# Two accumulators and two query banks in PSUM as four tiles, and a reciprocal written back to PSUM

## The chip, the cores and the metric

The kernel runs on one core of one Trainium2 chip. The metric is the device time of one execution in microseconds; for the kernel before, the median of three runs is 2843.22 us (2841.27 to 2845.21).

## The reference

One token of a small decoder, batch 2: an attention layer with a cache, a gated GELU layer, and both once more with the same weights, each on a layer norm of `x` and added back to `x`. All numbers are float32.

```python
def _A_ref(x, k_cache, v_cache, wq, wo):          # x (2,1,576), caches (2,32,8192,128)
    q = (x @ wq).reshape(B, Sq, H, Dh).transpose(0, 2, 1, 3)
    scores = jnp.einsum("bhqd,bhkd->bhqk", q, k_cache) * (Dh ** -0.5)
    p = _softmax(scores, axis=-1)
    o = jnp.einsum("bhqk,bhkd->bhqd", p, v_cache)
    return o.transpose(0, 2, 1, 3).reshape(B, Sq, H * Dh) @ wo

def _B_ref(x, w_gate, w_up, w_down):              # 576 -> 4608 -> 576
    h = _gelu(x @ w_gate) * (x @ w_up)
    return h @ w_down

x = x + _A_ref(_layernorm(x), ...)
x = x + _B_ref(_layernorm(x), ...)
x = x + _A_ref(_layernorm(x), ...)
x = x + _B_ref(_layernorm(x), ...)
```

The two caches have 268 MB each and are read once in each attention layer, so nearly all of the traffic is cache.

## The kernel before

**Items and slots.** The attention of a layer is a list of items. A *pair* item is two heads of one batch element (30 of them), a *single* is one head (4: s0 to s3). Layer 0 takes the pairs, then the singles; layer 1 goes backward, and takes some of the singles' keys and values from where layer 0 left them in SBUF. A pair's keys are one load of 128 partitions x 16384 numbers, its values another. SBUF holds three slots of that size (`P0`, `P1`, `P2`), and the loads go round them in turn: keys of item n, values of item n, keys of item n+1, and so on. So the values of item n take the slot of the keys of item n-1, and the keys of item n+1 the slot of the values of item n-1.

**Loads.** A small planner (`Space`) keeps a list of loads in a fixed order and issues the next one on the SP queue (line 136 for caches) as soon as the program has reached the instruction that frees its slot: the last sum over a slot of keys, or the last matmul over a slot of values. On the chip the SP queue then waits for that instruction. The order of the loads is the order of the list.

**One item.** `query(n)` (line 452, TensorE) spreads the item's query over the partitions into bank `n % 2` of the PSUM tile `qp`. `multiply(n, unit)` (line 480, VectorE) multiplies a unit of the keys with it in place; a pair has five units, of two, two, two, one and one eighths. GpSimd adds the two halves of each product (line 484), and VectorE sums what is left (`add_up`, line 490). `peak`, `highest`, `softmax` and `total` find the maximum (501, 503, 508, 511), the exponentials (519, 523, ScalarE) and their sum over the partitions, a matmul into the PSUM tile `tot` (533). `values(n)` (551, TensorE) multiplies the exponentials with the values into bank `n % 2` of the PSUM tile `acc`. `invert` (541, 543) makes the reciprocal of the sum and the weights, `gather` (561, 563) picks the diagonal of the accumulator, `context` (571, 576) applies the weights.

**Order.** The order on each engine is the program's (a manual schedule). For a pair it is, in the loop over units k:

```python
made = multiply(n, unit)
if k == 0:  query(n + 1)              # the next item's query, after the first multiply
else:       add_up(*pending)
if k == 2:  invert(n - 1)
if k == 3:  gather(n - 1); context(n - 1)
...
# after the last unit
add_up(*pending); peak(n); highest(n); softmax(n); total(n); values(n)
```

So on TensorE the query of item n+1 stands behind the values matmuls of item n-1, and on VectorE the work on item n-1 that needs the values matmuls stands behind the fourth multiply of item n. For singles, the end of one item lies inside the next. The framework sets the semaphores: it lets an instruction wait for another where both touch a tile in a way that it sees as a conflict.

**Other uses of the two tiles.** The query projection of a layer goes through `acc`, and the gate and up products of the GELU layer take both banks of `acc` for one half and both of `qp` for the other (662); `copy` takes one bank with ScalarE (672) and the other with VectorE (673).

Of the kernel before, what the change touches and what calls it, by code (L numbers as in the profile page):

```python
# [9 lines left out]
F32 = mybir.dt.float32  # L10
AF = mybir.ActivationFunctionType
ALU = mybir.AluOpType
# [3 lines left out]
P = 128  # L16
# [3 lines left out]
DH = 128  # L20
# [5 lines left out]
HALF = P // 2  # L26
# [3 lines left out]
WIN = 2 * RW  # L30
# [4 lines left out]
BF = CF // 2  # L35
# [60 lines left out]
def decode_layers(ctx, tc, x_in, kc, vc, wq, wo, wg, wu, wd, out):  # L96
    nc = tc.nc
# [3 lines left out]
    work = ctx.enter_context(tc.tile_pool(name="work", bufs=2))  # L101
    once = ctx.enter_context(tc.tile_pool(name="once", bufs=1))
    psum1 = ctx.enter_context(tc.tile_pool(name="psum1", bufs=1, space=PSUM))
# [3 lines left out]
    space = consts.tile([P, END], F32, name="space")  # L107
    sp = Space()
    at_of = {}
# [12 lines left out]
    def done(key):  # L122
        sp.free(key)
        sp.pump()
# [194 lines left out]
    prz = consts.tile([P, 2, 32, 2, 4], F32, name="prz")  # L319
# [9 lines left out]
    spread = consts.tile([P, 8, B], F32, name="spread")  # L329
    chosen = consts.tile([P, 2, B], F32, name="chosen")  # L330

    acc = psum1.tile([P, 2, 512], F32, name="acc")
    qp = psum1.tile([P, 2, 512], F32, name="qp")
    xps = psum1.tile([P, 512], F32, name="xps")
    nc.vector.tensor_scalar(x, x, onerow, None, op0=ALU.add)
    nc.vector.memset(xps, 0.0)
    for s in range(2):
        nc.vector.memset(acc[:, s, :], 0.0)
        nc.vector.memset(qp[:, s, :], 0.0)

    wide = x.rearrange("p (q i) -> p q i", i=9)

# [26 lines left out]
    def norm(apart):  # L369

        every = psum2.tile([P, B * 24], F32, name="every", tag="small")
        nc.tensor.matmul(every, ones, apart.rearrange("p b c t -> p (b c t)"), start=True, stop=True)
        mv = work.tile([P, B, 2], F32, name="mv")
        for b in range(B):
            nc.vector.bn_aggr(mv[:, b, :], every[:, 24 * b:24 * b + 24])
        ve = work.tile([P, B], F32, name="ve")
        nc.vector.tensor_scalar_add(ve, mv[:, :, 1], EPS)  # L377
        rstd = work.tile([P, B], F32, name="rstd")
        nc.gpsimd.tensor_tensor(out=rstd, in0=ve, in1=mhalf, op=ALU.pow)  # L379
        shift = work.tile([P, B], F32, name="shift")  # L380
        nc.vector.scalar_tensor_tensor(shift, mv[:, :, 0], -1.0, rstd, op0=ALU.mult, op1=ALU.mult)
        k8 = pick.rearrange("p c g r -> p (c g) r")
        part = work.tile([P, 8, B], F32, name="part")
        nc.vector.tensor_mul(spread, k8[:, :, 0:B], rstd.unsqueeze(1).to_broadcast([P, 8, B]))
        nc.vector.tensor_mul(
            part, k8[:, :, B:RW].to_broadcast([P, 8, B]), shift.unsqueeze(1).to_broadcast([P, 8, B])
        )
        nc.vector.tensor_add(spread, spread, part)
        nc.vector.reduce_sum(
            chosen.rearrange("p g b -> p (g b)"), spread.rearrange("p (c g) b -> p (g b) c", c=4), axis=AX.X  # L390
        )

    def window(g, i):
        at = RW * (1 - g) + 32 * i
        return xt[:, at:at + WIN]

    both = xm[:, 3:5, :].rearrange("p k r -> p (k r)")
    only = [xm[:, k:k + 2, :].rearrange("p k r -> p (k r)") for k in (0, 1)]


    def attention(layer, items, apart):
        last = len(items) - 1
        qsb = once.tile([P, CQ], F32, name="qsb", tag="row")

        def queries(bank, lhs, at, start, stop):
            for c in range(4):
                nc.tensor.matmul(
                    bank[32 * c:32 * c + WIN, :], lhs, space[:, at + c * CQ:at + (c + 1) * CQ],
                    start=start, stop=stop,
                )  # L410

        if layer == 0:
            bank = acc[:, 0, :]
            for off, n in ((0, 3), (3, 3), (6, 2)):
                for u in range(off, off + n):
                    queries(bank, window(u % 2, u // 2), at_of["wq", 0, off] + (u - off) * HQ, u == 0, False)
                done(("wq", 0, off))
                if off == 0:
                    norm(apart)
            queries(bank, both, at_of["wq", 0, "m"], False, True)  # L420
            done(("wq", 0, "m"))
            nc.scalar.activation(qsb, bank, AF.Copy)
        else:
            for i in range(NW):
                queries(acc[:, 1, :], window(1, i), at_of["wq", 1, 1, i], i == 0, False)
                done(("wq", 1, 1, i))
                if i == 0:
                    norm(apart)
            queries(acc[:, 1, :], only[1], at_of["wq", 1, "m"], False, True)
            queries(xps, only[0], at_of["wq", 1, "m"], True, False)  # L430
            done(("wq", 1, "m"))
            nc.scalar.activation(qsb, acc[:, 1, :], AF.Copy)

        def rest_of_queries():
            for i in range(NW):
# [7 lines left out]
        S, peaks, low, osb, weights = {}, {}, {}, {}, {}  # L443
# [3 lines left out]
        def query(n):  # L447
            item = items[n]
            for e in range(2):
                h = item.h + (e if item.heads == 2 else 0)  # L450
                half, c = h // 16, (h // 4) % 4
                nc.tensor.matmul(  # L452
                    qp[HALF * e:HALF * e + HALF, n % 2, 0:DH],
                    chosen[32 * c:32 * c + WIN, half, item.b:item.b + 1].to_broadcast([WIN, HALF]),
                    qsb[32 * c:32 * c + WIN, (h % 4) * DH:(h % 4 + 1) * DH], start=True, stop=True,
                )
# [11 lines left out]
        def multiply(n, unit):  # L468
            item = items[n]
            lo, hi = unit  # L470
            if lo == 0:
                S[n] = work.tile([P, 128], F32, name="S")
            j = 16 * (hi - lo)
            at = base_of("k", item, lo)
            t = space[:, at:at + (hi - lo) * PART].rearrange("p (j d) -> p j d", d=DH)
            u = t
            if layer == 0 and lo < stays("k", item):
                at = at_of["scratch", item.name] + lo % 2 * PART
                u = space[:, at:at + PART].rearrange("p (j d) -> p j d", d=DH)
            nc.vector.tensor_tensor(  # L480
                out=u, in0=t, in1=qp[:, n % 2, 0:DH].unsqueeze(1).to_broadcast([P, j, DH]), op=ALU.mult
            )
            half = u[:, :, :DH // 2]
            nc.gpsimd.tensor_tensor(out=half, in0=half, in1=u[:, :, DH // 2:], op=ALU.add)  # L484
            return n, unit, half
# [51 lines left out]

        def invert(n):
            heads = items[n].heads
            rinv = work.tile([P, heads], F32, name="rinv")  # L540
            nc.vector.reciprocal(rinv, low.pop(n))
            weights[n] = work.tile([P, heads], F32, name="weights")
            nc.vector.tensor_mul(weights[n], of[:, 0:2] if heads == 2 else of[:, 2:3], rinv)  # L543

        def values(n):
            item = items[n]
            groups = item.rows // 4
            for g in range(groups):
                c = g % 4
                at = base_of("v", item, g // 4) + g % 4 * 4 * DH  # L550
                nc.tensor.matmul(  # L551
                    acc[32 * c:32 * c + 8, n % 2, :], prz[:, n % 2, g, :, :].rearrange("p e r -> p (e r)"),
                    space[:, at:at + 4 * DH], start=(g < 4), stop=(g >= groups - 4),
                )
                if g % 4 == 3 and (layer == 1 or g // 4 >= stays("v", item)):
                    done(key_of("v", item, g // 4))

        def gather(n):
            t = osb[n] = work.tile([P, DH], F32, name="osb")
            q = acc[:, n % 2, :].rearrange("p (r d) -> p r d", r=4)  # L560
            nc.vector.tensor_scalar_mul(t, q[:, 0, :], diag[:, 0:1])
            for r in range(1, 4):
                nc.vector.scalar_tensor_tensor(t, q[:, r, :], diag[:, r:r + 1], t, op0=ALU.mult, op1=ALU.add)  # L563
# [89 lines left out]
    def mlp(layer, apart):  # L653
        banks = acc, qp
        done_first = set()

        def products(half, lhs, at, stop):
            for s in range(2):
                for c in range(4):
                    key = half, s, c  # L660
                    lo = at + c * CF + s * BF
                    nc.tensor.matmul(  # L662
                        banks[half][32 * c:32 * c + WIN, s, 0:BF], lhs, space[:, lo:lo + BF],
                        start=key not in done_first, stop=stop,
                    )
                    done_first.add(key)
# [2 lines left out]

        def copy(half):  # L670
            t = o[half] = once.tile([P, 2, BF], F32, name="o", tag="row")
            nc.scalar.activation(t[:, 0, :], banks[half][:, 0, 0:BF], AF.Copy)  # L672
            nc.vector.tensor_copy(t[:, 1, :], banks[half][:, 1, 0:BF])  # L673

        def turned(half):
            t = o[half].rearrange("p s w -> p (s w)")
# [32 lines left out]
        if layer == 0:  # L709
# [14 lines left out]
            d = downs[0]  # L724
# [63 lines left out]
```

## Time and profile before

| what | value |
|---|---|
| median of three runs | 2843.22 us (2841.27 to 2845.21) |
| the profiled execution, time / span | 2843.0 us / 2841.2 us |
| granted TensorE clock, mean | 0.637 |
| read from HBM | 1153.18 MB, 406 GB/s over the span |
| busy: VectorE / GpSimd / TensorE | 2002.7 / 1173.6 / 955.8 us |

Layer 0's pairs end near 1264 us of the span, its singles near 1352; then come the output projection, the GELU layer and the next query projection, to about 1474; layer 1's singles and pairs, to about 2757; and the last projection and GELU layer. In the rows of the profile PE is TensorE's matmul, PEld its weight load, DVE is VectorE, ACT ScalarE, POOL GpSimd and SPq the queue on which the loads are issued. A row of the timeline has the start in us, the duration in us, engine, line, operation, output and input by name, and in a bracket the time for which the engine stood idle before it and what released it. Tile names come without their numbers.

### The profile page before, as it was taken

How to read it: one execution, taken by the hardware profiler on the slowest of the kernel's cores; microseconds unless marked ns; L12 is line 12 of the kernel's file. 1: busy time of each engine (PE TensorE's matmuls, PEld its weight loads, DVE VectorE, ACT ScalarE, POOL GpSimd, SP SyncE). 2: the span in 40 equal slices, each digit the busy share in tenths (PEclk: the TensorE clock that was granted, in tenths of full speed). 3: DMA queues.
4: the chain of work that ended last, by engine and by line, in shares of the span. 5: the costliest groups of instructions: out<-in, count | busy, mean ns of one | idle time of the engine just before them, and what ended most of it. 6: DMA issues, size and time to landing. Idle time of an engine off the chain costs nothing.

```text
span 2841.2 us, 18902 instructions
## 1 busy us (share of the span) xinstructions
PE 955.8 (34%) x7836; PEld 347.6 (12%) x7836; DVE 2002.7 (70%) x1330; ACT 93.1 (3%) x419; POOL 1173.6 (41%) x342
## 2 busy tenths in 40 slices
PE   1332333233223322334654332332233223323345
PEld 0110011011101110111211110111011001100123
DVE  4678777877777787768029778777777877787760
ACT  0000000000000000000000000000000000000000
POOL 2444444444444344434015444444444444444430
PEclk7665666666566656666666656665666566666668
DMA  9999999999999999997999999999999999999999
GB/s 428 427 428 402 427 400 413 410 416 401 413 415 409 404 412 416 412 392 311 379 350 380 440 414 416 416 412 400 427 400 413 400 428 400 414 399 427 399 417 389
DMA packets 30853, 1154.39 MB, mean 406 GB/s; under 512 B 3488, under 2 KB 3504, under 8 KB 5296
## 3 DMA queue, kind: packets, MB, share of 16 engines
q1 hardware_dynamic: 30744, 1153.19, 95.9%
q8 instruction: 61, 1.00, 0.1%
q14 instruction: 24, 0.20, 0.0%
q10 hardware_dynamic: 24, 0.01, 0.0%
HBM read 1153.18 MB, written 0.00 MB: 406 GB/s over the span
## 4 chain that ended last, share of the span: by engine, by line
DVE 26%; PE 14%; DMA 7%; issue 5%; POOL 2%; ACT 1%; POOLq 0%; SPq 0%; DVEq 0%
DVE space L480 11%; PE acc L551 10%; DVE S L490 9%; DVE weights L543 3%; DMA space<-in_B_w_down_dram 3%; POOL space L484 2%; DMA space<-in_B_w_gate_dram 2%; DVE osb L563 1%; DMA space<-in_A_k_cache_dram 1%; PE nb L511 1%; ACT prz L523 1%; DMA space<-in_A_wo_dram 1%; PE tot L533 1%; DMA space<-in_B_w_up_dram 1%; PE qp L452 0%
## 5 line engine op out<-in xcount | busy, mean ns | idle before, releaser
L484 POOL TENSOR_TENSOR space<-space 128x2048 f32<-128x2048 f32 (+1 forms) x332 | 1170.1, 3525 | 1439.7 <-DVE space L480 1397.3
L480 DVE TENSOR_TENSOR space<-space,qp 128x4096 f32<-128x4096 f32 (+1 forms) x332 | 1140.9, 3437 | 511.3 <-PE qp L452 413.7
L490 DVE TENSOR_REDUCE S<-space 128x32 f32<-128x2048 f32 (+1 forms) x332 | 594.4, 1790 | 85.7 <-POOL space L484 85.7
L551 PE MATMUL acc<-space,prz 128*8 128x512 f32 x4096 | 595.9, 746 | 0.0
L571 PE MATMUL po<-weights,osb 128*32 128x1 f32 x1024 | 59.5, 201 | 1260.3 <-DVE osb L563 1260.3
L571 PEld LDWEIGHTS po<-weights,osb 128*32 128x32 f32 x1024 | 54.1, 154 | 1278.3 <-DVE osb L563 1278.1
L551 PEld LDWEIGHTS acc<-space,prz 128*8 128x8 f32 x4096 | 114.8, 104 | 419.2 <-issue 409.5
L503 PE MATMUL mT<-ident,m 128*1 128x128 f32 x68 | 25.1, 369 | 384.5 <-DVE m L501 384.5
L543 DVE TENSOR_TENSOR weights<-of,rinv 128x2 f32<-128x2 f32 (+1 forms) x68 | 149.5, 2199 | 2.4
L511 PE MATMUL nb<-m,strip 1*128 1x1 f32 x256 | 64.5, 350 | 38.8 <-DVE m L508 38.8
L576 ACT COPY oT<-po 64x4 f32<-64x4 f32 (+1 forms) x68 | 10.7, 157 | 2028.0 <-PE po L571 2028.0
L563 DVE SCALAR_TENSOR_TENSOR osb<-acc,diag,osb 128x128 f32<-128x128 f32 x204 | 71.6, 351 | 7.3
L379 POOL TENSOR_TENSOR rstd<-ve,mhalf 128x2 f32<-128x2 f32 x4 | 2.8, 699 | 167.2 <-DVE ve L377 167.2
L511 PEld LDWEIGHTS nb<-m,strip 1*128 1x128 f32 x256 | 58.7, 313 | 57.6 <-DVE m L508 54.6
L533 PE MATMUL tot<-rs,strip 128*128 128x2 f32 x120 | 34.9, 360 | 77.2 <-ACT prz L523 77.2
L503 PEld LDWEIGHTS mT<-ident,m 128*1 128x1 f32 x68 | 5.4, 79 | 397.4 <-DVE m L501 366.1
L523 ACT ACTIVATE prz<-S,nbs 64x128 f32<-64x128 f32 (+1 forms) x136 | 53.4, 393 | 3.1
L452 PE MATMUL qp<-qsb,chosen 6*64 6x128 f32 x272 | 31.3, 308 | 26.2 <-DVE space L480 25.5
L533 PEld LDWEIGHTS tot<-rs,strip 128*128 128x128 f32 x120 | 29.8, 308 | 82.3 <-ACT prz L523 82.3
L508 DVE TENSOR_REDUCE m<-mT 1x2 f32<-1x128 f32 (+1 forms) x68 | 18.9, 278 | 28.3 <-PE mT L503 28.3
L673 DVE COPY o<-acc 128x288 f32<-128x288 f32 x2 | 0.9, 458 | 53.0 <-ACT o L672 53.0
L662 PE MATMUL acc<-space,xt 128*6 128x288 f32 x256 | 28.9, 588 | 26.3 <-DMA space<-in_B_w_up_dram 15.4
(89 smaller groups left out, 336.6 us busy)
## 6 DMA issues: line engine op xcount, KB each, us to landing
space<-in_A_k_cache_dram SPq DMA_DIRECT2D x6, 4096.0 KB
space<-in_A_wo_dram SPq DMA_DIRECT2D x16, 1152.0 KB
space<-in_A_v_cache_dram SPq DMA_DIRECT2D x3, 4096.0 KB
space<-in_B_w_down_dram SPq DMA_DIRECT2D x13, 864.0 KB
space<-in_A_wq_dram SPq DMA_DIRECT2D x10, 1024.0 KB
space<-in_B_w_gate_dram SPq DMA_DIRECT2D x8, 1152.0 KB
space<-in_B_w_up_dram SPq DMA_DIRECT2D x8, 1152.0 KB
space<-in_B_w_gate_dram SPq DMA_DIRECT2D x2, 4608.0 KB
```

The lines of the kernel that those rows point to most:

```text
L452: nc.tensor.matmul(qp[HALF * e:HALF * e + HALF, n % 2, 0:DH], chosen[32 * c:32 * c + WIN, half, item.b:item.b + 1].to_broadcast([WIN, HALF ...
L480: nc.vector.tensor_tensor(out=u, in0=t, in1=qp[:, n % 2, 0:DH].unsqueeze(1).to_broadcast([P, j, DH]), op=ALU.mult)
L484: nc.gpsimd.tensor_tensor(out=half, in0=half, in1=u[:, :, DH // 2:], op=ALU.add)
L490: nc.vector.tensor_reduce(out=S[n][:, 16 * lo:16 * hi], in_=half, axis=AX.X, op=ALU.add)
L503: nc.tensor.transpose(peaks[n], m, ident)
L511: nc.tensor.matmul(low[n], one_of[e] if heads == 2 else ones[0:1, :], m1[:, e:e + 1], start=(e == 0), stop=(e == heads - 1),)
L523: nc.scalar.activation(prz[rows_, n % 2, 0:item.rows // 4, e, :], s[rows_, 0:item.rows].rearrange("p (g r) -> p g r", r=4), AF.Exp, bias=n ...
L533: nc.tensor.matmul(tot, ones, rs[:, n % 2, :], start=True, stop=True)
L543: nc.vector.tensor_mul(weights[n], of[:, 0:2] if heads == 2 else of[:, 2:3], rinv)
L551: nc.tensor.matmul(acc[32 * c:32 * c + 8, n % 2, :], prz[:, n % 2, g, :, :].rearrange("p e r -> p (e r)"), space[:, at:at + 4 * DH], start ...
L563: nc.vector.scalar_tensor_tensor(t, q[:, r, :], diag[:, r:r + 1], t, op0=ALU.mult, op1=ALU.add)
L571: nc.tensor.matmul(po[lo + 32 * e:lo + 32 * e + 32, n % 2, i:i + 1], t[:, i::GH], w[:, e:e + 1], start=True, stop=True,)
```

## The change

`acc` and `qp`, one tile of two banks each, become lists of two tiles of one bank each; every use takes the same bank as before under its new name. [...] The order of the program is untouched. Second, `invert` writes the reciprocal over the sum in PSUM in place of a tile in SBUF, and the weights are made from there. The core of the diff:

```diff
-    acc = psum1.tile([P, 2, 512], F32, name="acc")
-    qp = psum1.tile([P, 2, 512], F32, name="qp")
+    acc = [psum1.tile([P, 512], F32, name="acc%d" % s) for s in range(2)]
+    qp = [psum1.tile([P, 512], F32, name="qp%d" % s) for s in range(2)]
...
                 nc.tensor.matmul(
-                    qp[HALF * e:HALF * e + HALF, n % 2, 0:DH],
+                    qp[n % 2][HALF * e:HALF * e + HALF, 0:DH],
...
             nc.vector.tensor_tensor(
-                out=u, in0=t, in1=qp[:, n % 2, 0:DH].unsqueeze(1).to_broadcast([P, j, DH]), op=ALU.mult
+                out=u, in0=t, in1=qp[n % 2][:, 0:DH].unsqueeze(1).to_broadcast([P, j, DH]), op=ALU.mult
             )
...
             heads = items[n].heads
-            rinv = work.tile([P, heads], F32, name="rinv")
-            nc.vector.reciprocal(rinv, low.pop(n))
+            rinv = low.pop(n)
+            nc.vector.reciprocal(rinv, rinv)
             weights[n] = work.tile([P, heads], F32, name="weights")
             nc.vector.tensor_mul(weights[n], of[:, 0:2] if heads == 2 else of[:, 2:3], rinv)
...
                 nc.tensor.matmul(
-                    acc[32 * c:32 * c + 8, n % 2, :], prz[:, n % 2, g, :, :].rearrange("p e r -> p (e r)"),
+                    acc[n % 2][32 * c:32 * c + 8, :], prz[:, n % 2, g, :, :].rearrange("p e r -> p (e r)"),
...
-            q = acc[:, n % 2, :].rearrange("p (r d) -> p r d", r=4)
+            q = acc[n % 2].rearrange("p (r d) -> p r d", r=4)
...
-            nc.scalar.activation(t[:, 0, :], banks[half][:, 0, 0:BF], AF.Copy)
-            nc.vector.tensor_copy(t[:, 1, :], banks[half][:, 1, 0:BF])
+            nc.scalar.activation(t[:, 0, :], banks[half][0][:, 0:BF], AF.Copy)
+            nc.vector.tensor_copy(t[:, 1, :], banks[half][1][:, 0:BF])
```

More of the change, by code (lines that the diff above doesn't have):

```diff
@@ L337, in decode_layers @@
     for s in range(2):
-        nc.vector.memset(acc[:, s, :], 0.0)
-        nc.vector.memset(qp[:, s, :], 0.0)
+        nc.vector.memset(acc[s], 0.0)
+        nc.vector.memset(qp[s], 0.0)
     wide = x.rearrange("p (q i) -> p q i", i=9)
@@ L412, in attention @@
         if layer == 0:
-            bank = acc[:, 0, :]
+            bank = acc[0]
             for off, n in ((0, 3), (3, 3), (6, 2)):
@@ L424, in attention @@
             for i in range(NW):
-                queries(acc[:, 1, :], window(1, i), at_of["wq", 1, 1, i], i == 0, False)
+                queries(acc[1], window(1, i), at_of["wq", 1, 1, i], i == 0, False)
                 done(("wq", 1, 1, i))
@@ L428, in attention @@
                     norm(apart)
-            queries(acc[:, 1, :], only[1], at_of["wq", 1, "m"], False, True)
+            queries(acc[1], only[1], at_of["wq", 1, "m"], False, True)
             queries(xps, only[0], at_of["wq", 1, "m"], True, False)
             done(("wq", 1, "m"))
-            nc.scalar.activation(qsb, acc[:, 1, :], AF.Copy)
+            nc.scalar.activation(qsb, acc[1], AF.Copy)
         def rest_of_queries():
@@ L662, in products @@
                     nc.tensor.matmul(
-                        banks[half][32 * c:32 * c + WIN, s, 0:BF], lhs, space[:, lo:lo + BF],
+                        banks[half][s][32 * c:32 * c + WIN, 0:BF], lhs, space[:, lo:lo + BF],
                         start=key not in done_first, stop=stop,
```

## The prediction

> **What bounds the kernel now.** First the busy shares and the transfer queue on the page, then the lists of waits, then one attention item in the timeline, then the stages side by side.
>
> ```profile
> PE 955.8 (34%) x7836; PEld 347.6 (12%) x7836; DVE 2002.7 (70%) x1330; ACT 93.1 (3%) x419; POOL 1173.6 (41%) x342
> q1 hardware_dynamic: 30744, 1153.19, 95.9%
> ```
>
> The second line says that the 16 DMA engines hold a packet 95.9% of the span, which looks like a kernel bound by its transfers and nothing else. The list of waits (microseconds in total, times, longest) says that VectorE also stops often, and the SP queue's own list says what the loads wait for:
>
> ```profile
> DVE space L480 <- PE qp L452: 413.7, 62, 11.5
> DVE space L480 <- DMA space<-in_A_k_cache_dram: 97.4, 54, 22.9
> SPq L136 <- DVE m L501: 1631.1, 61, 29.3
> SPq L136 <- PE qp L452: 723.4, 56, 13.2
> ```
>
> In the multiply (L480) VectorE waits four times as long for the query matmul (L452) as for the keys. Whether that matters depends on whether loads are issued late. Here is one item, from the end of one to the end of the next; the bracket is the idle time before the row and its releaser.
>
> ```profile
> 607.79 0.33 SPq L136 DMA_DIRECT2D space<-in_A_v_cache_dram  x1
> 607.80 0.29 DVE L501 TENSOR_REDUCE m<-S 128x1 f32<-128x128 f32 x1
> 608.55 0.28 DVE L508 TENSOR_REDUCE m<-mT 1x2 f32<-1x128 f32 x1 [0.46 <-PE mT L503]
> 610.32 4.42 DVE L480 TENSOR_TENSOR space<-space,qp 128x4096 f32<-128x4096 f32 x1 [1.49 <-DMA space<-in_A_k_cache_dram]
> 611.18 0.58 PE L533 MATMUL tot<-rs,strip 128*128 128x2 f32 x2 [1.29 <-ACT prz L523]
> 611.70 9.22 PE L551 MATMUL acc<-space,prz 128*8 128x512 f32 x64
> 620.85 0.43 PE L452 MATMUL qp<-qsb,chosen 6*64 6x128 f32 x4
> 620.99 0.33 SPq L136 DMA_DIRECT2D space<-in_A_k_cache_dram  x1
> 621.33 4.42 DVE L480 TENSOR_TENSOR space<-space,qp 128x4096 f32<-128x4096 f32 x1 [6.58 <-PE qp L452]
> 632.44 4.50 POOL L484 TENSOR_TENSOR space<-space 128x2048 f32<-128x2048 f32 x1 [2.03 <-DVE space L480]
> 634.39 0.16 DVE L541 RECIPROCAL rinv<-tot 128x2 f32<-128x2 f32 x1
> 634.58 2.38 DVE L543 TENSOR_TENSOR weights<-of,rinv 128x2 f32<-128x2 f32 x1
> 641.28 0.34 DVE L561 TENSOR_SCALAR osb<-acc,diag 128x128 f32<-128x128 f32 x1
> 648.76 0.33 SPq L136 DMA_DIRECT2D space<-in_A_v_cache_dram  x1
> 651.39 4.42 DVE L480 TENSOR_TENSOR space<-space,qp 128x4096 f32<-128x4096 f32 x1 [1.59 <-DMA space<-in_A_k_cache_dram]
> ```
>
> Follow it. At 607.80 the keys of the previous item are summed. The softmax chain leads to the values matmuls (611.70 to 620.92); the query for the item *after* stands behind them on TensorE (620.85). VectorE has done this item's first multiply by 614.74, and its second multiply, which reads the other query bank, stops for 6.58 us until that query is written. From 621.33 VectorE runs on to 648.76, and only then is the next value load issued, because its slot was the keys' slot. So 13.53 us (607.80 to 621.33) plus 27.43 us (to 648.76) close a ring of 40.96 us through VectorE and TensorE. The load at 648.76 comes only 2.63 us before the keys ahead of it are used; the queue almost runs dry once an item. The stages show the price (window, its length, busy times with instruction counts, clock, DMA share, GB/s):
>
> ```profile
> 84.73:123.44 38.71, 8.75 (x71) 3.44 (x63) 30.81 (x19) 1.31 (x6) 18.23 (x5) 0.57 1.00 434
> 84.73:201.21 116.48, 29.98 (x239) 11.03 (x227) 92.44 (x54) 3.44 (x16) 54.73 (x15) 0.61 1.00 432
> 201.21:1224.00 1022.79, 308.87 (x2273) 107.10 (x2274) 770.78 (x451) 32.08 (x147) 456.26 (x125) 0.63 0.96 410
> 1224.00:1342.00 118.00, 48.75 (x329) 17.66 (x329) 96.39 (x81) 6.22 (x30) 55.84 (x21) 0.67 0.83 348
> 1342.00:1480.00 138.00, 89.22 (x1031) 32.93 (x1035) 17.40 (x60) 3.08 (x11) 4.87 (x4) 0.67 0.94 362
> 1480.00:1579.00 99.00, 43.78 (x247) 15.37 (x243) 87.59 (x72) 5.80 (x28) 52.42 (x20) 0.66 0.94 391
> 1695.95:2720.51 1024.56, 309.42 (x2275) 107.60 (x2275) 770.41 (x450) 33.49 (x154) 456.17 (x125) 0.62 0.97 410
> 2720.51:2841.20 120.69, 73.33 (x1075) 38.75 (x1075) 39.12 (x56) 2.69 (x12) 18.95 (x6) 0.78 0.95 404
> ```
>
> POOL runs five times an item, so the second row holds 3 items (15), the third and the seventh 25 each (125). In the second, with loads issued ahead, an item takes 116.48 / 3 = **38.83 us** at 432 GB/s and a DMA share of 1.00. In the two long ones it takes 1022.79 / 25 = 40.91 and 1024.56 / 25 = 40.98 us. The long stages are bound by the ring, not by the transfers.
>
> **Part 1: four PSUM tiles.** Instruction order is the same on every engine in the built program of the changed kernel. What differs is waits. With two banks in one tile, the second multiply waits for the write of the other bank, and that query waits for the first multiply; with separate tiles both waits are absent. The query's own reader, the next item's first multiply, comes some 25 us later. Without the 6.58 us stop, VectorE's round is 1.04 us (607.79 to the end of L508 at 608.83), 4.42 us (first multiply) and 27.43 us: 32.89 us. That is below 38.83, so the transfers become the bound. What is late next? The value load is then issued 38.83 - 4.42 - 27.43 = 7.0 us before the keys ahead of it are used. The key load waits for the values matmuls to free their slot; these end 13.13 us after the keys are summed (607.79 to 620.92), so it goes out 7.0 + 19.4 - 13.1 = 13.3 us before the values ahead of it have landed (19.4 us is half an item). Both leads exceed the 2.63 us of now. The two long stages give 25 x (40.91 - 38.83) = **52.0** and 25 x (40.98 - 38.83) = **53.8** us.
>
> A wait on TensorE is added at line 561 (the gather of the weighted values) and one at the reciprocal, since the second multiply no longer covers them. Behind line 561 stand the last multiply and sums, and so the value load. It costs nothing: the gather runs at 641.28, and the values matmuls it needs ended at 620.92, 20.4 us before; without the stop of 6.58 and the 2.2 us of part 2 some 11.6 us are left, and more once VectorE waits for keys.
>
> **Part 2: the reciprocal into PSUM.** The small multiply at L543 takes 2.38 us for 128x2 numbers: it begins at 634.58 and ends at 636.96, just when GpSimd's operation (632.44 + 4.50 = 636.94) ends. With GpSimd idle it is far shorter:
>
> ```profile
> 1345.26 0.16 DVE L543 TENSOR_TENSOR weights<-of,rinv 128x1 f32<-128x1 f32 x1
> ```
>
> Its form afterwards, one operand in SBUF and one in PSUM, is that of L480, which begins at 621.33 or 627.86 without such a delay. I take 0.16 us, so 2.22 us less a pair item and a round of 30.7 us; the other end is that it stays at 2.38. In the long stages either end is hidden by the transfers. [...]
>
> **Part 3: single-head items and the middle.** In the layer-0 singles VectorE alone sets the pace, so its stops are on the path to the first projection load:
>
> ```profile
> 1235.88 4.42 DVE L480 TENSOR_TENSOR space<-space,qp 128x4096 f32<-128x4096 f32 x1 [7.45 <-PE qp L452]
> 1276.77 2.29 DVE L480 TENSOR_TENSOR space<-space,qp 128x2048 f32<-128x2048 f32 x1 [10.23 <-PE qp L452]
> 1283.62 1.29 DVE L543 TENSOR_TENSOR weights<-of,rinv 128x2 f32<-128x2 f32 x1
> 1294.32 2.29 DVE L480 TENSOR_TENSOR space<-space,qp 128x2048 f32<-128x2048 f32 x1 [1.10 <-PE qp L452]
> 1341.94 1.28 SPq L186 DMA_DIRECT2D space<-in_A_wo_dram  x3
> 1535.86 0.33 SPq L136 DMA_DIRECT2D space<-in_A_v_cache_dram  x1
> ```
>
> From 1224.00 to 1341.94 are 117.94 us; without the three stops (18.78) 99.2; without the delays at L543 (one of 2.2, three of about 1.1) 93.6. The transfers of this window, 118.00 x 348 = 41.1 MB, need 95.1 us at 432 GB/s. The larger counts: 95.1, and 1 us for a value load that will just miss its turn, so **22** us. If L543 keeps its delay it is 99.2, and 3 us less is gained. The stage from 1342 runs at 362 GB/s on rings of small weight tiles that the change does not touch: 0, with 4 us either way. The start of layer 1 (391 GB/s, VectorE again ahead of the load at 1535.86) would take 99.00 x 391 / 432 = 89.6 us at full rate, 9.4 less; but only the L543 delays and the stop of about 1 us per single (1.10 above) go, so I take **5**, between 0 and 9. The last stage holds 0.95 and ends with what follows the last landing: 0, at most 1.
>
> The sum is made on the profiled execution, 2843.0 us (span 2841.2); the median of the runs shown is 0.2 higher, which I leave out. 52.0 + 53.8 + 22 + 5 = 132.8; 2843.0 - 132.8 = **2710 us**.
>
> **Rivals.** (a) *Only the idle share comes back.* If a packet takes as long as now, the long stages return 4% of 1022.79 and 3% of 1024.56, and the singles 17% of 118: 40.9 + 30.7 + 20.1, giving 2751. For it: busy share and rate in the third row give 410 / 0.96 = 427 GB/s while busy. Against it: the second row reached 432 with every engine at work.
> (b) *No change.* The wait could hide another that is as late, and the time stays 2843. Against it: the items of the second row did 38.83.
> (c) *Slower: the transfers lose their rate.* VectorE and GpSimd would work more densely while loads run. If that brought the loads down to 400 GB/s, about the lowest slice in these stages,
>
> ```profile
> GB/s 428 427 428 402 427 400 413 410 416 401 413 415 409 404 412 416 412 392 311 379 350 380 440 414 416 416 412 400 427 400 413 400 428 400 414 399 427 399 417 389
> ```
>
> an item, two loads of 128 x 16384 numbers of 4 bytes or 16.78 MB, would take 41.9 us, and 50 items 50 us more than now; the singles would take 102.7, 15 less: 2878. It decides below about 407 GB/s. Against it, the second row again; for it only that the dense state lasted 3 items there.
>
> **How the numbers follow.** Forecast 0.80, (a) 0.14, (b) 0.02, (c) 0.04. At the low end the item takes 38.71 us (the first row of the stages, one item at 434 GB/s), 6 us less, and layer 1's start and the middle give 6 more: 2698. At the high end stands (a), 2751, with 4 us for the middle: 2755. A measurement of this kernel tells 0.2% from nothing: faster by more 0.94, within 0.02, slower by more 0.04.
>
> **What would show it.** In the changed profile: L480 no longer waits for L452, but for the key load, some 8 us an item; the value load is issued some 9 us ahead of the first multiply; L543 near 0.16 us; DMA share 1.00 and about 432 GB/s in both long stages, 38.8 us an item. Wrong would be: a stop of VectorE at L561 or L541, or a DMA share of 1.00 at a rate below 425.

## The result and the profile after

The changed kernel took 2714.31 us (median of four runs, 2709.85 to 2719.83) against 2842.24 us before in the same comparison, a ratio of 0.955 with a 95% interval of 0.953 to 0.957. The forecast was 2710, between 2698 and 2755. The profiled execution took 2719.8 us, with a span of 2718.0; it is the slowest of the four.

The page of the changed kernel, busy shares and the transfer queue:

```profile
PE 956.4 (35%) x7836; PEld 346.4 (13%) x7836; DVE 1870.2 (69%) x1330; ACT 93.1 (3%) x419; POOL 1171.3 (43%) x342
q1 hardware_dynamic: 30744, 1153.19, 99.0%
```

VectorE is busy for 132.5 us less, almost what the span lost (123.2), but the two are not the same microseconds: the busy time is the delay at L543, and the experiments below show that the span falls nearly as far when that delay stays. The queue's share rose from 95.9% to 99.0%. From the lists of waits of the changed kernel, the engines' and then the SP queue's own:

```profile
DVE space L480 <- DMA space<-in_A_k_cache_dram: 467.7, 60, 23.9
DVE space L480 <- PE qp L452: 11.0, 1, 11.0
...
SPq L136 <- DVE m L501: 1515.5, 61, 29.2
SPq L136 <- PE acc L551: 779.5, 66, 14.8
```

The multiply's wait for the query matmul (413.7 us in 62 stops before) is down to one stop, the first multiply of layer 1, and its wait for keys has gone from 97.4 to 467.7 us. VectorE stands still about as long as before; it waits for something else. One item of the changed kernel in the timeline:

```profile
589.90 8.75 DVE L480 TENSOR_TENSOR space<-space,qp 128x4096 f32<-128x4096 f32 x2 [7.70 <-DMA space<-in_A_k_cache_dram]
594.67 0.43 PE L452 MATMUL qp<-qsb,chosen 6*64 6x128 f32 x4
594.81 0.33 SPq L136 DMA_DIRECT2D space<-in_A_k_cache_dram  x1
607.84 0.17 DVE L541 RECIPROCAL tot<-tot 128x2 f32<-128x2 f32 x1
608.04 0.16 DVE L543 TENSOR_TENSOR weights<-of,tot 128x2 f32<-128x2 f32 x1
612.65 0.34 DVE L561 TENSOR_SCALAR osb<-acc,diag 128x128 f32<-128x128 f32 x1
620.14 0.33 SPq L136 DMA_DIRECT2D space<-in_A_v_cache_dram  x1
624.04 8.53 PE L551 MATMUL acc<-space,prz 128*8 128x512 f32 x60
628.61 4.42 DVE L480 TENSOR_TENSOR space<-space,qp 128x4096 f32<-128x4096 f32 x1 [7.43 <-DMA space<-in_A_k_cache_dram]
```

The first two multiplies now stand in one row (x2): nothing comes between them, and the query of the next item is written meanwhile. L543 takes 0.16 us. The keys are summed at 620.14, and the value load issued there is 8.5 us ahead of the first multiply at 628.61, which uses the keys queued ahead of it. Below this time is called the lead of the value load. In the item shown of the kernel before it was 2.63 us; over the 25 items of layer 0's long stage the timelines give a median of 1.7 us before (1.4 to 3.1) and 8.5 now (8.1 to 9.6).

The stages, cut at the same events as before (first multiplies, the first projection load, the first key load of layer 1), with the length, busy times, clock, DMA share and GB/s:

```profile
201.38:1172.00 970.62, 306.71 (x2283) 106.88 (x2279) 717.70 (x451) 32.74 (x150) 455.12 (x125) 0.61 1.00 433
1172.00:1269.84 97.84, 44.12 (x300) 15.90 (x292) 89.87 (x80) 5.07 (x25) 55.88 (x21) 0.65 0.96 411
1269.84:1412.86 143.02, 93.00 (x1027) 32.75 (x1027) 17.23 (x59) 3.08 (x11) 4.84 (x4) 0.61 0.94 352
1412.86:1625.39 212.53, 83.33 (x528) 28.95 (x532) 169.45 (x130) 9.88 (x47) 107.14 (x35) 0.60 0.98 419
1625.39:2596.44 971.05, 305.68 (x2279) 106.62 (x2275) 717.72 (x450) 32.74 (x150) 455.18 (x125) 0.62 1.00 433
2596.44:2718.00 121.56, 68.80 (x1057) 37.54 (x1049) 37.01 (x56) 2.64 (x11) 18.93 (x6) 0.76 0.93 393
```

Both long stages run at 433 GB/s with a share of 1.00, at 970.62 / 25 = 38.82 and 38.84 us an item. For the third and the fourth stage the kernel before had, between the same events:

```profile
1341.94:1479.98 138.04, 89.20 (x1031) 32.93 (x1035) 17.43 (x60) 3.08 (x11) 4.84 (x4) 0.67 0.94 362
1479.98:1695.95 215.97, 75.58 (x498) 27.24 (x490) 181.14 (x129) 9.08 (x44) 107.18 (x35) 0.63 0.97 412
```

### The profile page after: what moved, and what is told of

Same layout as the page of the kernel before. It is cut to its first block, busy times and chain, and to the rows that moved or that the text cites. A ratio compares the mean times of both kernels' runs of the same rounds, so it can differ in the third digit from the quotient of the medians.

```text
span 2718.0 us, 18914 instructions
## 1 busy us (share of the span) xinstructions
PE 956.4 (35%) x7836; PEld 346.4 (13%) x7836; DVE 1870.2 (69%) x1330; ACT 93.1 (3%) x419; POOL 1171.3 (43%) x342
## 4 chain that ended last, share of the span: by engine, by line
DMA 24%; DVE 14%; PE 9%; POOL 6%; issue 1%; ACT 1%; POOLq 0%; SPq 0%; DVEq 0%
DMA space<-in_A_k_cache_dram 18%; DVE space L480 8%; POOL space L484 6%; PE acc L551 6%; DVE S L490 4%; DMA space<-in_B_w_down_dram 3%; DMA space<-in_B_w_up_dram 1%; DMA space<-in_B_w_gate_dram 1%; DVE osb L563 1%; PE nb L511 1%; ACT prz L523 1%; DMA space<-in_A_wo_dram 1%; DMA space<-in_A_wq_dram 1%; PE xps L703 0%; PE tot L533 0%
## 5 line engine op out<-in xcount | busy, mean ns | idle before, releaser
L480 DVE TENSOR_TENSOR space<-space,qp 128x4096 f32<-128x4096 f32 (+1 forms) x332 | 1136.1, 3437 | 478.7 <-DMA space<-in_A_k_cache_dram 467.7
L576 ACT COPY oT<-po 64x4 f32<-64x4 f32 (+1 forms) x68 | 10.7, 157 | 1898.2 <-PE po L571 1898.2
L662 PE MATMUL acc<-space,xt 128*6 128x288 f32 x256 | 31.3, 626 | 30.5 <-DMA space<-in_B_w_up_dram 15.0
L703 PE MATMUL xps<-space,hT 128*2 128x144 f32 x576 | 29.5, 370 | 13.9 <-DMA space<-in_B_w_down_dram 13.9
L561 DVE TENSOR_SCALAR osb<-acc,diag 128x128 f32<-128x128 f32 x68 | 23.3, 342 | 15.1 <-PE acc L551 15.1
```

Source lines behind the costliest of these rows:

```text
L480: nc.vector.tensor_tensor(out=u, in0=t, in1=qp[n % 2][:, 0:DH].unsqueeze(1).to_broadcast([P, j, DH]), op=ALU.mult)
L662: nc.tensor.matmul(banks[half][s][32 * c:32 * c + WIN, 0:BF], lhs, space[:, lo:lo + BF], start=key not in done_first, stop=stop,)
L703: nc.tensor.matmul(xps[32 * c:32 * c + B, 0:CW], hT[t // 2][:, i, t % 2, :], space[:, a:a + CW], start=(t == 0 and i == 0), stop=(t == NT ...
```

## The experiments

Theory: a ring of VectorE and TensorE (40.96 us an item), closed by a wait for a bank that the multiply does not read, was longer than the two loads of an item (38.8 us), and the transfers set the pace once it is opened. Rivals: that the gain belongs to one part alone, or that the time returned with VectorE's work.

**The changed kernel again.**

> The changed kernel once more, for the size of its own scatter. The theory of the ring: pairs at 38.8 us an item again, 2710 to 2720 us. The middle stage (first projection load to the first key load of layer 1) took 138.0 us before and 143.0 after, at a granted clock of 0.58 to 0.62 and of 0.50 over the gate and up products. If the lower clock sets it, a run with a higher clock there shows 138 to 140, one with a lower clock 143 or more; if the change itself lengthened it, it is 143 at any clock.

Measured: 2711.04 us (2708.27 to 2713.05), ratio 0.9527 (0.9513 to 0.9541), span of the profiled execution 2707.3. Layer 0's pairs again, and the middle stage:

```profile
201.20:1171.82 970.62, 307.04 (x2279) 106.88 (x2275) 717.54 (x450) 32.73 (x150) 455.14 (x125) 0.61 1.00 433
1269.29:1402.23 132.94, 89.96 (x1027) 32.93 (x1027) 16.16 (x58) 3.08 (x11) 3.72 (x3) 0.64 0.96 376
```

Layer 0's pairs are the same to the hundredth. The middle stage is ten microseconds shorter at nearly the same clock (0.64 against 0.61), so neither guess held. Over all profiles but that of the longer weight ring it lay between 131.8 (two sums more, clock 0.66) and 143.4 us (accumulators only, 0.62). The two longest, 143.0 and 143.4, go with 0.61 and 0.62, but 0.67 and 0.68 show 138, so the clock alone does not order it, nor does the edit. What moves it stays open. The spans of the two profiled executions differ by 10.7 us, and this stage by 10.1 of them.

**Query banks only.** The accumulators stay one tile, the reciprocal stays in SBUF.

```diff
-    qp = psum1.tile([P, 2, 512], F32, name="qp")
+    qp = [psum1.tile([P, 512], F32, name="qp%d" % s) for s in range(2)]
```

> Only the two query banks are separate tiles; accumulators joint, reciprocal in SBUF. Theory of the ring: without the stop at the second multiply VectorE's round is 32.9 us, under the 38.8 us of the transfers, so the pairs give back the whole 106 us; the delays at L543 stay (2.4 us an item) and cost only in the singles, about 3 us: 2715 to 2722. Rival, that the delay at L543 or the accumulators carry a good part of the gain: 2750 or more.

Measured: 2720.24 us (2718.84 to 2724.78), ratio 0.9563 (0.9549 to 0.9577). Its wait for the query, its pair stage of layer 0, and the small multiply (min/median/max in ns):

```profile
DVE space L480 <- PE qp L452: 12.8, 1, 12.8
...
200.97:1172.12 971.15, 310.15 (x2283) 107.30 (x2279) 771.02 (x450) 32.73 (x150) 455.29 (x125) 0.61 1.00 433
...
L543 DVE TENSOR_TENSOR weights<-of,rinv x68: 159/2378/2727, 102.9 to 2634.9; 128x2 f32<-128x2 f32 x60, 128x1 f32<-128x1 f32 x8
```

The delay at L543 is there in full (2378 ns) and VectorE is as busy as before (771.02 in this stage), yet the stops for the query are down from 62 to one and the pairs take 971 us: opening the ring at the query banks suffices. It also settles the rival that the time came back with VectorE's work.

**The reciprocal only.**

```diff
-            rinv = work.tile([P, heads], F32, name="rinv")
-            nc.vector.reciprocal(rinv, low.pop(n))
+            rinv = low.pop(n)
+            nc.vector.reciprocal(rinv, rinv)
```

> Only the reciprocal goes to PSUM; both tiles stay joint, so the second multiply still waits for the query. Theory of the ring: L543 lies in the 27.43 us that VectorE runs after the stop, so the ring of 40.96 becomes 38.74 us, just under the 38.83 of the transfers. Pairs at 38.8 to 39.2 us an item, the stop still there, total 2715 to 2755 (the singles keep their stops of 18.8 us). Rival, that the separate tiles are what counts and the 2.22 us are off the path: 2838 to 2846.

Measured: 2722.65 us (2720.76 to 2729.84), ratio 0.9577 (0.9559 to 0.9595). Both tiles are still joint, and the multiply still waits for the query; this is what its waits at L480 look like (us, times), with its pair stage and its L543:

```profile
  DMA space<-in_A_k_cache_dram: 446.7, 60
  PE qp L452: 70.3, 62
...
201.17:1171.93 970.76, 304.58 (x2279) 106.65 (x2275) 717.60 (x451) 32.74 (x150) 456.36 (x125) 0.62 1.00 433
...
L543 DVE TENSOR_TENSOR weights<-of,tot x68: 154/156/158, 103.2 to 2632.1; 128x2 f32<-128x2 f32 x60, 128x1 f32<-128x1 f32 x8
```

It still waits 62 times, but for 70 us in place of 414. Nothing was done to that wait: 2.22 us taken off at another place made the ring 38.74 us, no longer than the transfers, so VectorE no longer falls behind the keys item by item. How it fell behind can be seen in the first items of the kernel before:

```profile
123.44 4.42 DVE L480 TENSOR_TENSOR space<-space,qp 128x4096 f32<-128x4096 f32 x1 [5.33 <-DMA space<-in_A_k_cache_dram]
130.21 4.42 DVE L480 TENSOR_TENSOR space<-space,qp 128x4096 f32<-128x4096 f32 x1 [2.35 <-PE qp L452]
162.50 4.42 DVE L480 TENSOR_TENSOR space<-space,qp 128x4096 f32<-128x4096 f32 x1 [3.89 <-DMA space<-in_A_k_cache_dram]
170.94 4.42 DVE L480 TENSOR_TENSOR space<-space,qp 128x4096 f32<-128x4096 f32 x1 [4.02 <-PE qp L452]
201.21 4.42 DVE L480 TENSOR_TENSOR space<-space,qp 128x4096 f32<-128x4096 f32 x1 [1.81 <-DMA space<-in_A_k_cache_dram]
```

VectorE takes up the keys as they land, 38.7 to 39.1 us apart, while the second multiplies stand 40.7 us apart. So the wait for keys shrinks (5.33, 3.89, 1.81 us), the stop for the query grows, and once the lead is used up the loads are held to the ring's pace. With the reciprocal alone the wait for keys lies inside the 13.53 us that the ring needs for TensorE in any case, and the lead stays at 8.3 us (median). Together with the run before, this is the strongest support for the ring: each of two edits at different places of it, one of 2.22 us, or 5%, gives back the pairs' whole loss. The rival (2838 to 2846) falls.

**The accumulators only.**

```diff
-    acc = psum1.tile([P, 2, 512], F32, name="acc")
+    acc = [psum1.tile([P, 512], F32, name="acc%d" % s) for s in range(2)]
```

> Only the two accumulators are separate tiles. Theory of the ring: values of an item write one bank while the other has been read 11 us before (gather at 600.3 to 601.8, values from 611.7), so nothing waited for that and nothing is gained: 2838 to 2847, pairs at 40.9 us. Rival, that the accumulators' sharing holds up the values and through them the query: 2715 to 2800.

Measured: 2846.25 us (2840.5 to 2851.31), ratio 1.0001 (0.9991 to 1.0011).

```profile
DVE space L480 <- PE qp L452: 413.4, 62, 12.5
...
201.69:1225.65 1023.96, 309.51 (x2274) 107.10 (x2273) 770.53 (x451) 32.76 (x150) 456.49 (x125) 0.62 0.96 409
```

Wait and stage are those of the kernel before.

**All but the accumulators:**

> The changed kernel with the accumulators joint again (query banks separate, reciprocal in PSUM). Theory: the accumulators carry nothing, 2708 to 2722, pairs at 38.8 us. Rival, that they matter once the query no longer holds VectorE up: 2730 or more.

Measured: 2714.22 us (2712.55 to 2720.02), ratio 0.9544 (0.9528 to 0.956): the accumulators carry nothing here either.

**More work on VectorE.** The changed kernel, with some of the sums of a pair item done twice or three times. The output is the same.

```diff
-            nc.vector.tensor_reduce(out=S[n][:, 16 * lo:16 * hi], in_=half, axis=AX.X, op=ALU.add)
+            for _ in range({0: 2, 2: 2}.get(lo, 1) if item.heads == 2 else 1):
+                nc.vector.tensor_reduce(out=S[n][:, 16 * lo:16 * hi], in_=half, axis=AX.X, op=ALU.add)
```

Two sums more (as above) and five (`{0: 3, 2: 3, 4: 2}`):

> The changed kernel, with two of each pair item's sums on VectorE done twice (the first and the second, 2.28 us each; the output stays the same): 4.6 us more work an item on VectorE. Theory, the transfers bound the pairs now and VectorE has 7.4 us an item to spare: pairs stay at 38.8 us, VectorE's wait for keys falls from 7.4 to about 2.9 us; the last pair of a layer ends 4.6 us later, so 2713 to 2725 in all. Rival, VectorE still sets the pace through when it frees the slots: 60 x 4.6, 2990 us.

> As the run before, with five sums more in each pair item (the first two twice more, the third once more): 11.4 us more on VectorE. VectorE's round is then 30.24 + 1.04 + 11.4 = 42.7 us, over the 38.8 us of the transfers by 3.9: pairs at 42.7 us, some 54 items times 3.9 and 11 us at the end of a layer's pairs, 2920 to 2950. Rival, that slack is larger because sums wait for GpSimd anyway: 2715 to 2800.

Then, since two sums cost more than was expected, one (`{0: 2}`) and three (`{0: 2, 2: 2, 4: 2}`):

> The changed kernel with the first sum of each pair item done twice (2.28 us more on VectorE an item; same output). With no sum more the value load goes out 8.5 us before the keys ahead of it are used (a wait of 7.4 us and 1.04 us) and an item takes 38.8 us; with two sums more it went out some 4.2 us before, and an item took 39.3 us at 427 GB/s though VectorE still waited for keys. Theory, a load that is queued late leaves the packets at the seam slower, and the loss begins somewhere between: at a lead of some 6.2 us an item takes 38.8 to 39.0 us, 2710 to 2722 in all. Rival, VectorE's extra reads slow the packets in proportion, whatever the lead: half of the 26 us, 39.05 us an item and 2722 to 2730.

> As the run before with the first three sums of each pair item done twice (6.84 us more). VectorE's round is 30.24 + 1.04 + 6.84 = 38.1 us, 0.7 under the transfers' 38.8, and the lead falls to some 2 us. Theory of the seam: an item takes 39.5 to 41 us, as the lead is short again as it was before the change (1.6 to 2.6 us), 2750 to 2830 in all. Rival, in proportion to the extra work: three times 13 us, 2745 to 2755, 39.5 us an item.

Measured: one sum 2713.59 us, ratio 0.9539 (0.9525 to 0.9553); two 2739.27, 0.963 (0.9615 to 0.9644); three 2797.62, 0.9832 (0.9812 to 0.9851); five 2947.71, 1.0359 (1.0344 to 1.0375). Layer 0's pairs, 25 items each (POOL x125), with one, two, three and five sums:

```profile
200.99:1172.05 971.06, 305.23 (x2279) 106.65 (x2275) 774.78 (x475) 32.73 (x150) 455.61 (x125) 0.62 1.00 433
...
201.59:1184.16 982.57, 308.29 (x2279) 107.05 (x2275) 829.71 (x500) 32.73 (x150) 455.94 (x125) 0.61 1.00 427
...
204.99:1207.12 1002.13, 309.92 (x2276) 106.98 (x2275) 886.82 (x526) 32.75 (x150) 456.44 (x125) 0.61 0.98 419
...
213.72:1280.83 1067.11, 308.07 (x2275) 107.09 (x2275) 998.69 (x576) 32.75 (x150) 456.76 (x125) 0.60 0.92 393
```

One sum is free: 38.84 us an item, with 57 us more VectorE work in the stage. Five make VectorE the bound: 42.68 us an item, as its round of 30.24 + 1.04 + 11.4 = 42.7 says. Two and three are between, at 39.30 and 40.09 us, though VectorE's round (35.8 and 38.1 us) is under 38.8 and it still waits for keys. My first theory had two sums free as well and missed by 14 us (2739.27 against 2725 at most). What goes with the loss is the lead of the value load. From the timelines of this stage, as medians: 8.5 and 6.1 us cost nothing, 4.4 us (3.9 to 5.7) costs 0.5 us an item, 3.0 us (1.7 to 4.2) costs 1.3. VectorE's work alone does not do it: with the query banks only, it was as busy as in the kernel before (771.02 and 770.78 us), but the lead was 6.4 us in place of 1.7, and the stage ran at 433 GB/s in place of 410. That the lead is the cause, and not only what goes with it, is not shown. The rival, in proportion to the work, expected 2722 or more for one sum and 2755 or less for three, and falls at both.

**A longer weight ring** (this ring is a buffer in SBUF that the weight tiles go round, not the ring of waits above), the changed kernel with four tiles in place of three in flight between the attention layers. The core of the diff; small tiles other than `apart` move to `once` as well:

```diff
-END = 24 * PART + 768
-MID = 21 * PART
+END = 24 * PART + 1024
+MID = 20 * PART
...
-    kept = {("k",) + s3.name: 4, ("k",) + s2.name: 4, ("k",) + s1.name: 1,
+    kept = {("k",) + s3.name: 4, ("k",) + s2.name: 4, ("k",) + s1.name: 0,
...
-    scratch(s1.name, P2, 1)
...
-    for k in range(1, 4):
+    for k in range(0, 4):
...
-        apart = work.tile([P, B, 4, 6], F32, name="apart")
+        apart = once.tile([P, B, 4, 6], F32, name="apart")
```

> The changed kernel, with a longer ring for the weights between the attention layers: one part of keys of a single (1 MB) is no longer kept from layer 0 to layer 1 but read again, the ring grows from 6912 to 9216 columns, so it holds four gate or up tiles in place of three; small normalization tiles give up their second buffer to make room. Theory, the middle stage (143 us at 352 GB/s) is bound by the ring's turn, in which a load waits for the products three tiles before: with four it comes near 432 GB/s, 143 becomes 120 to 130, and 2.4 us go for the extra read: 2692 to 2708. Rival, the loads of 1.2 MB are slow by themselves (387 to 399 GB/s at a DMA share of 1.00): 2710 to 2720.

Measured: 2698.36 us (2697.92 to 2699.8), ratio 0.9483 (0.9469 to 0.9497). Its middle stage, from the same events; then the stretch in it from the first gate load to the first load of `w_down`; then the same stretch in the run with the reciprocal only, which had the same clock there:

```profile
1268.41:1394.31 125.90, 85.96 (x1043) 31.93 (x1043) 20.47 (x61) 3.09 (x11) 6.88 (x5) 0.73 0.98 404
1288.15:1338.39 50.24, 35.01 (x382) 12.45 (x382) 4.73 (x24) 0.80 (x3) 0.70 (x1) 0.67 1.01 421
...
1302.11:1357.00 54.89, 35.15 (x366) 11.88 (x366) 4.73 (x24) 0.80 (x3) 0.71 (x1) 0.67 0.99 392
```

It beats both kernels; its interval lies below that of the changed kernel (0.9513 to 0.9541). The stage takes 125.9 us, less than in any of the other profiles (131.8 to 143.4), and runs at 404 GB/s. Its clock is the highest too (0.73), but in the stretch of the gate and up loads, at the same clock of 0.67, it is 4.65 us shorter than in the other run; in the second profile of the changed kernel the stretch took 52.73 us at a clock of 0.57. So part of what the stage lacked was the weight ring's turn; how much of the rest is the clock or the stage's own scatter is open.

## Why the prediction was right

The ring and what opens it, the next bound (transfers at 38.83 us; measured 38.82 and 38.84) and the delay at L543 all came as worked out; in the item shown VectorE waits 7.4 us for keys (forecast some 8), and the lead is 8.5 us (some 9), as its round without waits is 31.3 us (30.24 + 1.04) and not 30.7. Term by term, expected and measured in the profiled execution: pairs of layer 0 52.0, and 1022.79 - 970.62 = 52.2; pairs of layer 1 53.8, and 53.5; singles of layer 0 22, and 117.94 - 97.84 = 20.1; the middle 0 (4 either way), and -5.0; start of layer 1 5, and 3.4; the end 0, and -0.9. In all 132.8, and 123.2. About half of the missing 9.6 us is the middle stage of that run. In the second profile, where that stage took 132.9, the span is 2707.3, against the 2708.4 (2841.2 - 132.8) that the forecast meant. That this is so near is partly luck: the middle stage gained 5.1 us there, which nothing foresaw, and that made up for some 4 us by which the singles and what follows the middle were taken too high. In both profiles the middle lies outside the 4 us that were allowed for it, so that term was mis-sized, and the cause is open.

The step that was off in its reason, though small in its size, is that the added waits cost nothing; a stop at L561 was one of the signs that would show the working wrong. At line 561 the kernel before had three waits, the changed kernel four (us, times), none of them in the steady stages:

```profile
  PE acc L551: 14.3, 3
...
  PE acc L551: 15.1, 4
...
1215.97 0.35 DVE L561 TENSOR_SCALAR osb<-acc,diag 128x128 f32<-128x128 f32 x1 [3.06 <-PE acc L551]
```

Two of the four stand where the kernel before has them too, behind the last item of a layer (5.70 and 8.35 us before, 4.85 and 6.64 now). New are one of 0.53 us and the row shown. That row is the gather that lies in the first single of layer 0, where VectorE, no longer stopped, arrives before the values are done: 3.06 of the 10.23 us of that stop came back at the next place that needs TensorE. The singles' 20.1 in place of 22 fit that; it was not measured by itself. The waits at L541 are two, as before.

On the rivals. (a), only the idle share comes back, falls: packets did get faster, from 427 GB/s while busy to 433. (b) falls by the result, (c) by the 433 GB/s of the long stages. The choice at L543, 0.16 us against 2.38, was right, by the two separate runs above: the median L543 takes 156 ns with one operand in SBUF and one in PSUM (the reciprocal only), and 2378 ns with both in SBUF (the query banks only). The traces of the two kernels show where the long ones stand. Of the 68 in the kernel before, the 66 that begin while a GpSimd operation runs take 1.22 to 2.38 us and end within 0.03 us of its end; the two that begin with GpSimd idle take 0.16. In the changed kernel 66 begin beside GpSimd as well, and all 68 take 0.155 to 0.157 us. A source in PSUM shows no cost: the shortest L543 is 159 ns with both operands in SBUF and 154 with one in PSUM, in the same two runs.

The working gave the pairs' gain to Part 1 and called Part 2 hidden there. That holds, but the reverse holds as well: in one comparison against 2844.43 us the query banks alone gave 124.2 us, the reciprocal alone 121.8, and all of the change 133.4. The parts do not add, since both take the same ring below the transfers. What the second adds lies for the most part in the singles: those of layer 0 took 117.9 us before, 102.1 with the banks alone, 106.5 with the reciprocal alone and 97.5 to 97.8 with all of the change.

## What to carry to other kernels

A transfer queue that is 96% busy may still be waiting for a compute ring: look for the stage where the loads are issued only just in time, and compare its time for an item with that of a stage where they are issued ahead. Follow the ring of waits around once and add it up; a cut that brings it under the next bound gave the whole gain in the stages that it bounds, and a second cut gave nothing more there. Being under the bound is not enough by itself: VectorE rounds of 35.8 and 38.1 us against transfers of 38.8 still cost 0.5 and 1.3 us an item, with loads issued 4.4 and 3.0 us ahead. Where two buffers take turns, look whether anything waits for the one that it does not touch, and make those two tiles: it gave 124 us for the query banks and nothing for the accumulators.

## What had not been expected of the hardware

For loads of 8.4 MB it was not enough to be queued in time: with a median lead of 6.1 us or more over the use of the load ahead an item ran at 433 GB/s; at 4.4 us 427, with the DMA share still 1.00; at 3.0 us 419. In all stages with a short lead the rate while busy comes out alike: 427 at 1.00, 419 / 0.98 = 428, 410 / 0.96 = 427 in the kernel before, 393 / 0.92 = 427 with five sums. So, within the rounding of the shares, the packets take longer there by some 1.4% whatever the lead, and the rest of the loss is an idle queue; why the packets take longer is open. And the middle stage of one and the same program took 143.0 us in one execution and 132.9 in another, at granted clocks of 0.61 and 0.64, where layer 0's pairs repeated to 0.01 us.
